# Square roots of the first six norm groups on GpSimd, by a power, in place of a logarithm and an exponential on ScalarE

## The chip, the cores and the metric

The kernel runs on one core of one Trainium2 chip. A core has five engines that work beside each other, each with its own queue of instructions that it takes in order: TensorE (PE: matmuls; its weight loads are listed apart as PEld), VectorE (DVE), ScalarE (ACT), GpSimd (POOL) and SyncE (SP, here only an issuer of DMAs). They wait for each other through semaphores. The metric is the time of one execution on the device in microseconds, lower is better; it is given as the median of three runs.

## The reference

Cosine attention, then a feed-forward layer with an exact GELU. There are 8 batches, 12 heads, 448 positions and a head dimension of 64, all in float32; `tau` is 0.1.

```python
q_n = q / (np.linalg.norm(q, axis=-1, keepdims=True) + 1e-06)
k_n = k / (np.linalg.norm(k, axis=-1, keepdims=True) + 1e-06)
scores = np.matmul(q_n, k_n.transpose(0, 1, 3, 2)) / tau
attn = exp(scores - max) ; attn = attn / (np.sum(attn, axis=-1, keepdims=True) + 1e-09)
x = (attn @ v), heads side by side          # 3584 tokens x 768
out = gelu(x @ w_in) @ w_out                # w_in 768 x 2048, w_out 2048 x 768
```

The change concerns the first two lines: the square root in the norm of each row of q and k.

## The kernel before

**Tiling.** Four heads of one batch make a group `g` of the attention; there are 24, three to a batch. A group's q and k are loaded as one tile `qk` of 128 partitions x (q or k, head pair, 7 chunks, 64). The norms are made in units: unit 0 and unit 1 are the two head pairs of group 0, and unit u above that is group u - 1 (line 116). Units are put together in norm groups n (line 118): norm groups 0 to 4 are units 0 to 4, and norm group 5 is units 5 and 6 together. So a norm group has 14 norms in each partition for n = 0 and 1, 28 for n = 2, 3 and 4, and 56 for n = 5.

**The norm chain.** For each unit: `load_qk` (DMA), `square` (on ACT in the opening, later on POOL), `reduce` (DVE sums 64 squares into `nq`), `logs` and `roots` (ACT: `lq` = Ln(nq + 1e-30), then Exp(0.5 lq) into every second column of a tile `root`, whose other column holds 1e-6), `inverses` (DVE adds the two columns into `se` and takes the reciprocal `rn`), `scale` (POOL multiplies q or k by `rn` into `qkb`, bf16), `transposes` (PE through PSUM for units 0 to 4, and then `copies` by DVE into `qkT`; one DMA from SP's queue for later units). Then `scores` (PE, `st`), `exps` (ACT, `pt`), `sums` and `values` (PE), and `normalise` (DVE) into `x`.

**The rest.** `mm` multiplies `x` by `w_in` into PSUM (`hp`), `gelu` (ACT) writes `g`, and `run` takes the next piece of the product of `g` and `w_out` (`op`), 16 steps over the hidden dimension to an output tile. The weights `wi` and `wo` and the values `v` are loaded by DMAs that POOL issues, so these issues stand in POOL's queue among the multiplications.

**What sets the order.** The function `opening` (line 538) writes out by hand the order of all work of the first three batches: each call in it appends its instructions to the queue of its engine, in this order, and an engine never passes an instruction that waits. For the batches after that, `first` and `attention` do the same by rules; the change does not touch them. [...] Logarithm and exponential share one set (`EXP_SET`) and the GELU has another (`GELU_SET`); `table` puts a table load in ACT's queue. In the opening the logs and roots of norm groups 0 to 4 stand where `EXP_SET` is loaded anyway, and those of norm group 5 stand inside the GELUs of batch 0, between a load of `EXP_SET` and a load of `GELU_SET` (lines 770 to 775).

PE runs a few matmuls that compute nothing (`spin`) in the opening. PSUM tiles of `mm_tile` come from two banks by turns; the transposes of unit 4 and the `hp` tiles 14 and 11 of batch 0 use the same two banks one after the other.

Of the kernel before, what the change touches and what calls it, by code (L numbers as in the profile page):

```python
# [9 lines left out]
F32 = mybir.dt.float32  # L10
BF16 = mybir.dt.bfloat16
AF = mybir.ActivationFunctionType
ALU = mybir.AluOpType
# [3 lines left out]
def kernel(  # L17
# [17 lines left out]
    nc = tc.nc  # L35
    B, H, S, D = q.shape
    C = S // D
# [10 lines left out]
    consts = ctx.enter_context(tc.tile_pool(name="consts", bufs=1))  # L48
# [34 lines left out]
    nc.vector.memset(ones2[64:128, :, 1], 1.0)  # L83
    tiny = consts.tile([128, 1], F32)
    nc.vector.memset(tiny, 1e-30)
    g_first = gp.tile([128, KF, 2 * S], BF16, tag="g", name="g0")
    blank = g_first[:, 0, :S]
    nc.vector.memset(blank, 0.0)

    root2 = [consts.tile([128, 4 * C, 2], F32, name=f"root2_{n}") for n in range(2)]  # L90
# [7 lines left out]
    EXP_SET = "natural_log_exp_and_others"  # L98
    GELU_SET = "gelu_and_others"
# [18 lines left out]
    groups = [[n] for n in range(NQ + 2)] + [[NQ + 2, NQ + 3], [2 * NQ + 1], [2 * NQ + 2]]  # L118
# [3 lines left out]
    shapes = [[len(gr), 2, units[gr[0]][2] - units[gr[0]][1], C] for gr in groups]  # L122
    place = {u: (n, j) for n, gr in enumerate(groups) for j, u in enumerate(gr)}
    qk_t, v_t, sq_t, nq_t, rn_t, qkb_t, qkT_t, pt_t = {}, {}, {}, {}, {}, {}, {}, {}
# [17 lines left out]
    def load_v(n):  # L142
        g, m = v_parts[n]
        t = vp.tile([128, m, 2, C, D], BF16, tag="v", name=f"v{g}")
        for j in range(m):
            v_t[g + j] = t[:, j]
        v_quads(t, g, 0, 1 if g == NQ else m)
        if g == NQ:
            v_rest.append((t, g, 1, m))
# [27 lines left out]
    def reduce(u, part=None):  # L177
        g, s0, s1 = units[u]
        n, j = place[u]
        if n not in nq_t:  # L180
            nq_t[n] = nrm.tile([128, len(groups[n]), 2, s1 - s0, C], F32, tag="nq", name=f"nq{n}")
        for i in range(2) if part is None else (part,):
            nc.vector.tensor_reduce(nq_t[n][:, j, i], sq_t[g, i][:, s0:s1], mybir.AxisListType.X, ALU.add)  # L183

    ln_t, sr_t = {}, {}

    def logs(n):
        nq = nq_t.pop(n)
        ln_t[n] = nrm.tile(list(nq.shape), F32, tag="lq", name=f"lq{n}")
        nc.scalar.activation(ln_t[n], nq, AF.Ln, bias=tiny)  # L190

    def roots(n):
        ln = ln_t.pop(n)
        sr_t[n] = root2[2 if len(groups[n]) == 2 else n % 2][:, :math.prod(shapes[n])]
        nc.scalar.activation(sr_t[n][:, :, 0], ln.rearrange("p j i s c -> p (j i s c)"), AF.Exp, scale=0.5)  # L195
# [10 lines left out]
    def root(n):  # L206
        logs(n)
        roots(n)
        inverses(n)

    def scale(u, parts=None):
        g, s0, s1 = units[u]
        n, j = place[u]
        rn = rn_t[n][:, j]
        if g not in qkb_t:
            qkb_t[g] = qkbp.tile([128, 2, C, 2, D], BF16, tag="qkb", name=f"qkb{g}")
        qkb, t = qkb_t[g], qk_t[g]
        for eng, i in parts or ((nc.gpsimd, 0), (nc.gpsimd, 1)):
            eng.tensor_tensor(  # L219
                qkb[:, i, :, s0:s1].rearrange("p c s d -> p s c d"), t[:, i, s0:s1],  # L220
                rn[:, i].to_broadcast([128, s1 - s0, C, D]), ALU.mult)
# [3 lines left out]
    def transposes(u, i=None):  # L225
        g, s0, s1 = units[u]
        qkb = qkb_t[g]
        if g not in qkT_t:
            qkT_t[g] = qkTp.tile([128, 2, C, 128], BF16, tag="qkT", name=f"qkT{g}")
        if i is None:  # L230
            nc.sync.dma_start_transpose(out=qkT_t[g].rearrange("p i c s -> p (i c) s"),
                                        in_=qkb.rearrange("p i c s d -> p (i c s d)"))
            return
        tp = tp_t[u, i] = mm_tile(f"tp{u}_{i}", (128, C, 128), BF16)
        for c in range(C):
            nc.tensor.transpose(tp[64 * s0:64 * s1, c, :], qkb[:, i, c, s0:s1].rearrange("p s d -> p (s d)"), ident)  # L236

    def copies(u, i):
        g, s0, s1 = units[u]
        rows = slice(64 * s0, 64 * s1)  # L240
        nc.vector.tensor_copy(qkT_t[g][rows, i], tp_t.pop((u, i))[rows])
# [5 lines left out]
    def scores(g, banks, p=None):  # L247
        qkT = qkT_t[g]
        if p is None:
            p = st_turn[0]  # L250
            st_turn[0] ^= 1
        st = pair(p, f"st{g}_{banks[0][1]}")
        for n, (s, c) in enumerate(banks):
            rows = slice(64 * s, 64 * (s + 1))
            for h in range(2):
                cols = slice(64 * h, 64 * (h + 1))
                nc.tensor.matmul(st[cols, n, :S], lhsT=qkT[rows, 1, c, cols], rhs=qkT[rows, 0, :, cols],  # L257
                                 start=True, stop=True, tile_position=(64 * s, 64 * h))
        st_t[g, banks[0]] = st
# [56 lines left out]
    def sums(g, chunks=range(C), p=None):  # L316
        for c in chunks:
            if c == 0:
                bank_t[g, "sm"] = ps_acc.tile([128, 512], F32, tag="sm", name=f"sm{g}") if g < NQ else \
                    pair(p, f"sm{g}")[:, 0]  # L320
            for s in range(2):
                if g < NQ:
                    nc.tensor.matmul(bank_t[g, "sm"][64 * s:64 * (s + 1), :S],  # L323
                                     lhsT=ones2.rearrange("p a h r -> p (a h r)"), rhs=pt_t[g, s, c],
                                     start=(c == 0), stop=(c == C - 1), tile_position=(0, 64 * s))
                    continue

                half = 2
                for i in range(2) if c == half else ((c - (c > half)) % 2,):
                    r = 32 * (2 * s + i)  # L330
                    cols = slice(i * S // 2, (i + 1) * S // 2) if c == half else slice(0, S)
                    nc.tensor.matmul(bank_t[g, "sm"][r:r + 32, cols], lhsT=ones, rhs=pt_t[g, s, c][:, cols],  # L332
                                     start=(c < 2), stop=(c >= C - 2), tile_position=(0, r))

    def values(g, chunks=range(C), p=None):
        for c in chunks:
            if c == 0 and g < NQ and p is None:
                bank_t[g, 0] = ps_acc.tile([128, 512], F32, tag="o", name=f"o{g}_0")
                bank_t[g, 1] = mm_tile(f"o{g}_1")
            elif c == 0:  # L340
                o = pair(p, f"o{g}")
                bank_t[g, 0], bank_t[g, 1] = o[:, 0], o[:, 1]
            for s in range(2):
                for h in range(2):
                    rows, cols = slice(64 * h, 64 * (h + 1)), slice(64 * s, 64 * (s + 1))
                    nc.tensor.matmul(bank_t[g, h][cols, :S], lhsT=v_t[g][rows, s, c, :],  # L346
                                     rhs=pt_t[g, s, c][rows], start=(c == 0), stop=(c == C - 1),
                                     tile_position=(64 * h, 64 * s))
# [113 lines left out]
    def load_wi(i):  # L462
        n = min(i, NQ - 1)
        half = d_ff // 2
        cols = slice(0, d_ff) if n < NQ - 1 else slice((i - n) * half, (i - n + 1) * half)
        for s in range(2):
            nc.gpsimd.dma_start(
                out=wi[64 * s:64 * (s + 1), 2 * n:2 * n + 2, cols],
                in_=moe_w_in[:, cols].rearrange("(n s h d) f -> n s d h f", s=2, h=2, d=D)[n, s])
# [30 lines left out]
    def table(name):  # L500
        nc.scalar.preload_act_table_set(name)
# [5 lines left out]
    def bank(b, m):  # L507
        hps_t[b, m] = mm_tile(f"hp{b}_{m}")[:, :S]
# [11 lines left out]
    def gelu(b, m):  # L520
        sb, hf = divmod(b, 2)
        nc.scalar.activation(g_t[sb][:, m, hf * S:(hf + 1) * S], hps_t.pop((b, m)), AF.Gelu)  # L522
# [15 lines left out]
    def opening():  # L538
# [11 lines left out]
        reduce(0, K)  # L550
        square(1, ((AC, Q),))
        load_v(0)
        logs(0)
        reduce(1, Q)
        roots(0)
        load_wi(0)
        square(1, ((AC, K),))
        inverses(0)
        square(2, ((AC, Q),))
        reduce(1, K)  # L560
        scale(0, ((GP, 1),))
        logs(1)
        reduce(2, Q)
        roots(1)
        scale(0, ((GP, 0),))
        spin(2)
        transposes(0, 1)
# [15 lines left out]
        load_v(1)  # L583
        transposes(1, 1)
        copies(1, 0)
        logs(2)
        scores(0, ((0, 2), (0, 3)))
        roots(2)
        load_wi(1)
        exps(0, ((0, 0), (0, 1)))  # L590
        inverses(2)
# [17 lines left out]
        sums(0, (0,))  # L609
        copies(2, 0)  # L610
        scores(0, ((1, 4), (1, 5)))
        logs(3)
        scores(0, ((0, 6), (1, 6)))
        roots(3)
        transposes(2, 1)
        exps(0, ((1, 4), (1, 5)))
        inverses(3)
# [97 lines left out]
        square(6, ((GP, Q),))  # L715
        reduce(5, Q)
        reduce(4, Q)
        logs(4)
        sums(2, (4,))
        sums(2, (5,))  # L720
        sums(2, (6,))
        roots(4)
        values(2, (5,))
        values(2, (6,))
        banks(0, 2, 0)
# [41 lines left out]
        load_wo(2)  # L767
        gelu(0, 1)
        bank(0, 14)
        table(EXP_SET)  # L770
        reduce(6, K)
        reduce(5, K)
        logs(5)
        roots(5)
        table(GELU_SET)
        gelu(0, 12)
        gelu(0, 10)
        inverses(5)
# [657 lines left out]
```

## Time and profile before

| | us |
|---|---|
| median of 3 runs | 391.75 (391.03 to 391.83) |
| span of the profiled execution | 390.6 |
| PE busy in the span | 382.6 (98%) |
| DVE busy | 273.0 (70%) |
| ACT busy | 269.9 (69%) |
| POOL busy | 248.7 (64%) |

The profile is of one execution; its span runs from its first to its last instruction, and it is the only time that is recorded for that execution. What a run's time holds beyond it is taken as the difference between the median and the span. A line of a timeline gives the start and the duration in us, the engine and the source line, the operation, the tile written and the tiles read, the shape, how many instructions are merged, and in brackets how long the engine had been idle and what ended it.

### The profile page before, as it was taken

The page shows a single profiled execution, that of the slowest core. Times are in us where ns is not written, and L with a number is a line of the kernel's source. Part 1 is how long each engine was busy: PE and PEld are TensorE (multiplying, and loading weights), DVE is VectorE, ACT ScalarE, POOL GpSimd, SP SyncE. Part 2 cuts the span into 40 slices and gives each one's busy share as a digit, 9 for nine tenths or more (in the row PEclk, how much of TensorE's full clock was granted, in tenths as well). Part 3 has the DMA queues.
Part 4 walks back from the last instruction along what each step waited for, and adds up shares of the span by engine and source line. Part 5 has one row for each costly group of instructions (what it writes and reads, how often), then busy time and mean ns, then how long its engine had stood idle before and what let it go on. Part 6 is the DMA issues. An engine that isn't in the chain of part 4 may idle for free.

```text
span 390.6 us, 13166 instructions
## 1 busy us (share of the span) xinstructions
PE 382.6 (98%) x5820; PEld 236.6 (61%) x5820; DVE 273.0 (70%) x509; ACT 269.9 (69%) x391; POOL 248.7 (64%) x161
## 2 busy tenths in 40 slices
PE   7899999999999999999999999999999999999996
PEld 3444568555777656865567556775567555655674
DVE  4878439876778896879696896889685993670032
ACT  5895789857999958996678767997577646504300
POOL 4796950557998399969594794969595770910000
PEclk9999999999999999999999999999999999999999
DMA  8999999926899691889067490876045600130033
GB/s 265 264 262 229 176 191 329 254 56 157 179 203 299 112 217 69 185 158 275 5 172 130 120 243 2 185 131 118 3 91 81 154 9 2 44 82 2 7 79 83
DMA packets 64473, 54.85 MB, mean 140 GB/s; under 512 B 38688, under 2 KB 60320, under 8 KB 64416
## 3 DMA queue, kind: packets, MB, share of 16 engines
q1 hardware_dynamic: 54464, 41.79, 42.0%
q0 software_dynamic: 9568, 11.80, 18.5%
q8 instruction: 45, 0.74, 0.8%
q10 hardware_dynamic: 384, 0.43, 0.4%
q14 instruction: 12, 0.10, 0.1%
HBM read 45.61 MB, written 11.01 MB: 145 GB/s over the span
## 4 chain that ended last, share of the span: by engine, by line
PE 95%; DMA 2%; SPq 1%; ACT 1%; issue 0%; DVE 0%; ACTq 0%
PE hp L493 37%; PE op L427 36%; PE st L257 9%; PE o L346 8%; DMA qk<-in_k_dram 2%; PE op L451 1%; PE sm L323 1%; PE sm L332 1%; PE tp L236 1%; SPq L134 1%; ACT sq L173 0%; ACT pt L267 0%; PE spin L489 0%; DVE last L454 0%; ACT root L195 0%
## 5 line engine op out<-in xcount | busy, mean ns | idle before, releaser
L427 PE MATMUL op<-wo,g 64*64 64x384 bf16 x3456 | 167.1, 323 | 0.2 <-issue 0.2
L267 ACT ACTIVATE pt<-st 128x896 bf16<-128x896 f32 x168 | 147.2, 918 | 19.6 <-PE st L257 17.5
L493 PE MATMUL hp<-x,wi 128*128 128x448 bf16 x768 | 147.0, 353 | 0.0
L427 PEld LDWEIGHTS <-g 64*64 64x64 bf16 x3456 | 106.2, 107 | 40.9 <-issue 4.2
L493 PEld LDWEIGHTS <-wi 128*128 128x128 bf16 x768 | 74.3, 98 | 71.6 <-issue 3.2
L219 POOL TENSOR_TENSOR qkb<-qk,rn 128x896 bf16<-128x896 f32 (+1 forms) x49 | 80.4, 1662 | 46.0 <-DVE rn L203 37.9
L278 POOL TENSOR_TENSOR acc<-acc,pt 128x896 f32<-128x896 f32 x55 | 103.8, 1888 | 4.3
L436 DVE TENSOR_REDUCE ot<-op 128x384 f32<-128x768 f32 x50 | 47.3, 946 | 54.7 <-PE op L427 47.5
L1357 ACT ACTIVATE g<-hp 128x448 bf16<-128x448 f32 x96 | 46.2, 547 | 55.1 <-PE hp L493 55.1
L257 PE MATMUL st<-qkT 64*64 64x448 bf16 x672 | 62.8, 352 | 0.5 <-ACT pt L267 0.5
L183 DVE TENSOR_REDUCE nq<-sq 128x14 f32<-128x896 f32 (+1 forms) x50 | 50.4, 1036 | 13.6 <-ACT sq L173 7.1
L380 DVE TENSOR_TENSOR x<-o,rs 128x448 bf16<-128x448 f32 x48 | 27.6, 611 | 22.9 <-PE o L346 21.9
L175 POOL TENSOR_TENSOR sq<-qk 128x896 f32<-128x896 f32 x16 | 26.6, 1685 | 23.8 <-DMA qk<-in_q_dram 13.3
L346 PE MATMUL o<-pt,v 64*64 64x448 bf16 x672 | 39.5, 349 | 0.0
L290 DVE TENSOR_TENSOR acc<-acc,pt 128x896 f32<-128x896 f32 x30 | 33.0, 1099 | 1.0
L173 ACT ACTIVATE sq<-qk 128x896 f32<-128x896 f32 (+1 forms) x33 | 28.8, 901 | 4.4 <-DMA qk<-in_q_dram 3.2
L257 PEld LDWEIGHTS <-qkT 64*64 64x64 bf16 x672 | 23.1, 106 | 11.7 <-issue 3.7
L375 DVE STREAM_TRANSPOSE rs<-rc 128x448 f32<-128x448 f32 x48 | 28.1, 621 | 0.4
L278 POOL TENSOR_TENSOR acc<-pt 128x896 f32<-128x896 bf16 x11 | 20.7, 1878 | 10.9 <-ACT pt L267 10.9
L346 PEld LDWEIGHTS <-v 64*64 64x64 bf16 x672 | 21.1, 107 | 9.2 <-issue 0.2
L522 ACT ACTIVATE g<-hp 128x448 bf16<-128x448 f32 x32 | 15.4, 547 | 12.8 <-PE hp L493 12.7
L295 DVE TRANSPOSE_TENSOR_REDUCE sa<-acc 128x28 f32<-128x896 f32 x17 | 18.8, 1104 | 0.2
(54 smaller groups left out, 176.0 us busy)
## 6 DMA issues: line engine op xcount, KB each, us to landing
qk<-in_q_dram SPq DMA_DIRECT2D x23, 448.0 KB, 4.9
qk<-in_k_dram SPq DMA_DIRECT2D x23, 448.0 KB, 5.8
out_dram<-ot SPq DMA_DIRECT2D x48, 192.0 KB, 4.0
v<-in_v_dram POOLq DMA_DIRECT2D x6, 672.0 KB, 7.2
wo<-in_moe_w_out_dram POOLq DMA_DIRECT2D x4, 768.0 KB, 10.6
wi<-in_moe_w_in_dram POOLq DMA_DIRECT2D x4, 512.0 KB, 13.8
out_dram<-ot SPq DMA_DIRECT2D x12, 96.0 KB, 2.1
wi<-in_moe_w_in_dram POOLq DMA_DIRECT2D x4, 256.0 KB, 14.1
```

The costliest lines, as they stand in the source:

```text
L173: eng.activation(sq, t, AF.Square)
L183: nc.vector.tensor_reduce(nq_t[n][:, j, i], sq_t[g, i][:, s0:s1], mybir.AxisListType.X, ALU.add)
L219: eng.tensor_tensor(qkb[:, i, :, s0:s1].rearrange("p c s d -> p s c d"), t[:, i, s0:s1], rn[:, i].to_broadcast([128, s1 - s0, C, D]), ALU. ...
L257: nc.tensor.matmul(st[cols, n, :S], lhsT=qkT[rows, 1, c, cols], rhs=qkT[rows, 0, :, cols], start=True, stop=True, tile_position=(64 * s, 6 ...
L267: nc.scalar.activation(pt, st[:, :, :S], AF.Exp, scale=inv_tau)
L278: nc.gpsimd.tensor_tensor(acc_t[g], all_t[g][:, 0] if c == 1 else acc_t[g], all_t[g][:, c], ALU.add)
L290: nc.vector.tensor_tensor(acc_t[g], acc_t[g], all_t[g][:, c], ALU.add)
L346: nc.tensor.matmul(bank_t[g, h][cols, :S], lhsT=v_t[g][rows, s, c, :], rhs=pt_t[g, s, c][rows], start=(c == 0), stop=(c == C - 1), tile_po ...
L427: nc.tensor.matmul(ps[cols, r, :NH], lhsT=g_t[sb][rows, kf, t * 128 + 64 * c:t * 128 + 64 * (c + 1)], rhs=wo[rows, kf, ni * NH:(ni + 1) * NH],
L436: nc.vector.tensor_reduce(part, ps[:, :, :NH].rearrange("p r d -> p d r"), mybir.AxisListType.X, ALU.add)
L493: nc.tensor.matmul(t, lhsT=wi[:, kd, m * 128:(m + 1) * 128], rhs=x_t[b][:, kd, :], start=(kd == 0), stop=(kd == KD - 1))
L1357: nc.scalar.activation(g_t[sb][:, m, hf * S:(hf + 1) * S], hps.pop(m), AF.Gelu)
```

## The change

The norm groups 0 to 5 get their roots by a new function `powers`, which is one POOL instruction: `nq` raised to the power of a constant tile `halves` that holds 0.5, written to the same column of the same `root` tile. The calls of `logs` and `roots` for these groups go, and with those of norm group 5 the two table loads around them. `powers(n)` stands where `roots(n)` stood. Norm groups 6 and later keep the logarithm and the exponential.

```diff
+    halves = consts.tile([128, 8 * C], F32)
+    nc.vector.memset(halves, 0.5)
...
+    def powers(n):
+        nq = nq_t.pop(n)
+        m = math.prod(shapes[n])
+        sr_t[n] = root2[2 if len(groups[n]) == 2 else n % 2][:, :m]
+        nc.gpsimd.tensor_tensor(sr_t[n][:, :, 0], nq.rearrange("p j i s c -> p (j i s c)"), halves[:, :m], ALU.pow)
...
         load_v(0)
-        logs(0)
         reduce(1, Q)
-        roots(0)
+        powers(0)
         load_wi(0)
...
         scale(0, ((GP, 1),))
-        logs(1)
         reduce(2, Q)
-        roots(1)
+        powers(1)
         scale(0, ((GP, 0),))
...
-        logs(2)
         scores(0, ((0, 2), (0, 3)))
-        roots(2)
+        powers(2)
         load_wi(1)
...
-        logs(3)
         scores(0, ((0, 6), (1, 6)))
-        roots(3)
+        powers(3)
...
-        logs(4)
         sums(2, (4,))
         sums(2, (5,))
         sums(2, (6,))
-        roots(4)
+        powers(4)
...
         bank(0, 14)
-        table(EXP_SET)
         reduce(6, K)
         reduce(5, K)
-        logs(5)
-        roots(5)
-        table(GELU_SET)
+        powers(5)
```

POOL's queue in the opening, from the first load of `v` to the scales of unit 3 (group 2), before the change; `rn` with another number is that of another norm group:

```order
L155 DMA v_180<-in_v_dram 128x2x448
L467 DMA wi<-in_moe_w_in_dram 64x2x2048 x2
L219 TENSOR_TENSOR qkb_197<-qk_133,rn_192 128x7x64 x2
L219 TENSOR_TENSOR qkb_197<-qk_133,rn_221 128x7x64 x2
L155 DMA v_260<-in_v_dram 128x4x448
L467 DMA wi<-in_moe_w_in_dram 64x2x2048 x2
L219 TENSOR_TENSOR qkb_297<-qk_139,rn_285 128x2x7x64 x2
L219 TENSOR_TENSOR qkb_364<-qk_142,rn_360 128x2x7x64
```

The same place with the change (the new lines of code move the line numbers by 2 to 8):

```order
L157 DMA v_182<-in_v_dram 128x2x448
L198 TENSOR_TENSOR root_0_127<-nq_178,halves 128x14
L475 DMA wi<-in_moe_w_in_dram 64x2x2048 x2
L227 TENSOR_TENSOR qkb_197<-qk_135,rn_192 128x7x64
L198 TENSOR_TENSOR root_1_128<-nq_184,halves 128x14
L227 TENSOR_TENSOR qkb_197<-qk_135,rn_192 128x7x64
L227 TENSOR_TENSOR qkb_197<-qk_135,rn_219 128x7x64 x2
L157 DMA v_258<-in_v_dram 128x4x448
L198 TENSOR_TENSOR root_0_127<-nq_199,halves 128x28
L475 DMA wi<-in_moe_w_in_dram 64x2x2048 x2
L227 TENSOR_TENSOR qkb_293<-qk_141,rn_281 128x2x7x64 x2
L198 TENSOR_TENSOR root_1_128<-nq_295,halves 128x28
```

Four powers have come into the queue: one ahead of the first `wi` issues, one between the two halves of the first scale, one ahead of the second `wi` issues, and one behind the scales that the third made possible.

POOL's queue further on, at batch 0's `hp` matmuls, before the change: two loads of `wo` in a row, between the scales of unit 4 and those of units 6 and 5.

```order
L175 TENSOR_TENSOR sq_0_631<-qk_319 128x896
L175 TENSOR_TENSOR sq_1_691<-qk_319 128x896
L219 TENSOR_TENSOR qkb_726<-qk_168,rn_697 128x2x7x64 x2
L473 DMA wo<-in_moe_w_out_dram 128x4x768 x2
L219 TENSOR_TENSOR qkb_815<-qk_319,rn_786 128x2x7x64
```

With the change:

```order
L177 TENSOR_TENSOR sq_0_625<-qk_315 128x896
L198 TENSOR_TENSOR root_0_127<-nq_567,halves 128x28
L177 TENSOR_TENSOR sq_1_683<-qk_315 128x896
L227 TENSOR_TENSOR qkb_718<-qk_170,rn_689 128x2x7x64 x2
L481 DMA wo<-in_moe_w_out_dram 128x4x768
L198 TENSOR_TENSOR root_0_129<-nq_627,halves 128x56
L481 DMA wo<-in_moe_w_out_dram 128x4x768
L227 TENSOR_TENSOR qkb_803<-qk_315,rn_774 128x2x7x64
```

The power of norm group 4 stands between the squares of unit 6, and that of norm group 5 between the two loads of `wo`. DVE's and PE's queues keep their order; on ACT twelve activations and two table loads are gone.

## The prediction

> **What bounds the kernel now.** I read the page first, then the busy time by stages, then each engine's timeline of the opening. The page says that TensorE (PE) is almost never idle.
>
> ```profile
> span 390.6 us, 13166 instructions
> PE 382.6 (98%) x5820; PEld 236.6 (61%) x5820; DVE 273.0 (70%) x509; ACT 269.9 (69%) x391; POOL 248.7 (64%) x161
> ```
>
> A share over the whole span hides where the idle lies, so the same by stages (start:end, length, then busy us and count of each engine, granted clock, DMA share, GB/s):
>
> ```profile
> 0.00:15.00 15.00, 10.84 (x64) 5.08 (x66) 8.41 (x27) 9.23 (x17) 8.72 (x18) 1.00 0.92 269
> 15.00:33.30 18.30, 18.29 (x235) 8.36 (x235) 14.80 (x25) 17.09 (x22) 17.07 (x14) 1.00 1.09 256
> 33.30:52.00 18.70, 18.70 (x116) 9.93 (x116) 8.64 (x16) 12.01 (x22) 15.54 (x11) 1.00 1.09 194
> 52.00:380.00 328.00, 327.81 (x5337) 208.32 (x5340) 238.89 (x440) 231.55 (x332) 207.36 (x119) 1.00 0.56 127
> ```
>
> PE loses 4.2 us in the first 15 us and 0.2 us in the next 365. Two things follow. After 15 us nothing that ScalarE (ACT) is relieved of can shorten the kernel unless PE's own queue gets going earlier; and a delay that reaches PE early is not made up later, since there is no idle time to eat it. From 15 to 33 us ACT is nearly as full as PE. Its timeline (start, duration, instruction, idle before):
>
> ```profile
> 13.52 0.30 ACT L190 ACTIVATE lq<-nq,tiny 128x28 f32<-128x28 f32 x1
> 13.85 0.23 ACT L195 ACTIVATE root<-lq 128x28 f32<-128x28 f32 x1
> 13.99 4.13 ACT L267 ACTIVATE pt<-st 128x896 bf16<-128x896 f32 x5
> 17.97 0.35 ACT L190 ACTIVATE lq<-nq,tiny 128x28 f32<-128x28 f32 x1
> 18.35 0.23 ACT L195 ACTIVATE root<-lq 128x28 f32<-128x28 f32 x1
> 18.48 1.71 ACT L267 ACTIVATE pt<-st 128x896 bf16<-128x896 f32 x2
> 20.35 12.07 ACT L267 ACTIVATE pt<-st 128x896 bf16<-128x896 f32 x14 [0.16 <-PE st L257]
> ```
>
> The fourteen exponentials of attention groups 1 and 2 run from 20.35 to 32.42 without a gap, so when the first of them starts decides when PE comes to the dense `hp` matmuls at 33.3 us. The two log and root pairs ahead of them cost ACT 13.99 - 13.52 = 0.47 and 18.48 - 17.97 = 0.51 us (each from the log's start to the next exponential's). Now GpSimd (POOL) in the same stretch:
>
> ```profile
> 5.77 0.89 POOL L155 DMA_DIRECT2D v<-in_v_dram  x1
> 6.65 1.22 POOL L467 DMA_DIRECT2D wi<-in_moe_w_in_dram  x2
> 7.86 1.86 POOL L219 TENSOR_TENSOR qkb<-qk,rn 128x448 bf16<-128x448 f32 x2
> 10.86 1.83 POOL L219 TENSOR_TENSOR qkb<-qk,rn 128x448 bf16<-128x448 f32 x2 [1.15 <-DVE rn L203]
> 12.64 0.83 POOL L155 DMA_DIRECT2D v<-in_v_dram  x1
> 13.46 1.20 POOL L467 DMA_DIRECT2D wi<-in_moe_w_in_dram  x2
> 14.84 3.33 POOL L219 TENSOR_TENSOR qkb<-qk,rn 128x896 bf16<-128x896 f32 x2 [0.19 <-DVE rn L203]
> 19.39 1.69 POOL L219 TENSOR_TENSOR qkb<-qk,rn 128x896 bf16<-128x896 f32 x1 [1.21 <-PE tp L236]
> ```
>
> POOL is the engine that makes the scaled q and k, which PE must transpose, and it is nearly full: from 10.86 to 18.17 it pauses for 0.19 us. The change puts the roots into this queue, in order, where ACT had run them beside it.
>
> **What one power costs.** No row shows a power on any engine. The nearest rows are POOL's own multiplications in two sizes (count, busy us, mean ns of one):
>
> ```profile
> L219 POOL TENSOR_TENSOR qkb<-qk,rn 128x896 bf16<-128x896 f32 x45 | 76.7, 1726 | 44.9 <-DVE rn L203 36.8 <-ACT pt L267 6.5 <-PE tp L236 1.2
> ...
> L219 POOL TENSOR_TENSOR qkb<-qk,rn 128x448 bf16<-128x448 f32 x4 | 3.7, 951 | 1.1 <-DVE rn L203 1.1
> ```
>
> Their difference gives (1726 - 951) / 448 = 1.73 ns an element, and 951 - 775 = 0.18 us fixed. Call the power's time a for 14 elements, b for 28, c for 56. The lower bound is a power at the price of one multiplication: a 0.20, b 0.23, c 0.28. Upwards I count steps: a power is a logarithm, a product and an exponential, each a chain of multiplications and additions, with range handling. As an estimate I take 30 such steps at 1.73 ns, 52 ns an element: a = 0.18 + 0.73 = 0.91, b = 1.64, c = 3.09. My upper bound is 70 steps, 121 ns: a 1.87, b 3.57, c 6.96. The count of steps is a choice; the multiplication's own price is the cheap end, and I leave it because a power can't be one multiplication.
>
> [...]
>
> **The sum, step by step.** Norm groups 0 and 1 (14 elements each). On POOL the first power stands behind the v load and before the two wi issues, so `scale(0)` of k starts at 7.86 + a; the second power stands between the two halves of `scale(0)`. Both halves and both powers end at 9.72 + 2a. `scale(1)` then had 1.15 us to wait for its reciprocal, and this pause takes in 2a up to 1.15. What is left is d = max(0, 2a - 1.15) = 0.67 us. On VectorE (DVE) `inverses(1)` waits for the second power, with the copies of attention group 0's transposes queued behind it; this ends before the pause does.
>
> Norm groups 2 and 3 (28 each). From the end of `scale(1)` POOL has: v issue to 13.46 + d, the power b, wi issues 1.20, `scale(2)` 3.33, the power b again. Sum: 13.46 + 1.20 + 3.33 = 17.99, plus d + 2b. Before, ACT ended this last root at 18.35 + 0.23 = 18.58. So the root of norm group 3 comes d + 2b - 0.59 = 0.67 + 3.28 - 0.59 = 3.36 us later. The 0.59 is what POOL loses in waits today. Who waits for that root:
>
> ```profile
> 18.61 0.21 DVE L201 TENSOR_REDUCE se<-root 128x28 f32<-128x56 f32 x1 [0.34 <-ACT root L195]
> 18.93 0.33 DVE L203 RECIPROCAL rn<-se 128x28 f32<-128x28 f32 x1
> 19.17 0.60 DVE L241 COPY qkT<-tp 128x896 bf16<-128x896 bf16 x1
> ```
>
> ```profile
> 19.91 0.71 PE L257 MATMUL st<-qkT 64*64 64x448 bf16 x8
> ```
>
> DVE works in order: `inverses(3)` holds the copy of attention group 1's second transpose, and the copy's end at 19.77 releases that group's first scores at 19.91, which release the run of fourteen exponentials. There is no slack in this chain, so all 3.36 us pass to ACT at 20.35 and to PE at 33.3. What ACT saves, 0.47 + 0.51 us, only lets attention group 0's exponentials end sooner; then ACT waits. `inverses(2)` likewise holds a copy for attention group 0's later scores, but by b + d, less than what follows.
>
> Norm group 4 (28). Its power stands between two squares, ahead of a pause for data:
>
> ```profile
> 34.25 1.68 POOL L175 TENSOR_TENSOR sq<-qk 128x896 f32<-128x896 f32 x1 [0.97 <-DVE rc L371]
> 38.00 1.68 POOL L175 TENSOR_TENSOR sq<-qk 128x896 f32<-128x896 f32 x1 [2.08 <-DMA qk<-in_k_dram]
> ```
>
> The pause takes in 2.07 us, more than b: nothing, and POOL even comes b - 2.07 = -0.43 us back against PE's shift. If b exceeded it, POOL would be that much later still.
>
> Norm group 5 (56 elements) and the two table loads. The power stands between the two issues of the last wo loads.
>
> ```profile
> 42.92 1.56 POOL L473 DMA_DIRECT2D wo<-in_moe_w_out_dram  x2
> ```
>
> ```profile
> 43.43 0.27 DVE L201 TENSOR_REDUCE se<-root 128x56 f32<-128x112 f32 x1 [1.64 <-ACT root L195]
> 43.74 0.50 DVE L203 RECIPROCAL rn<-se 128x56 f32<-128x56 f32 x1
> 47.13 1.15 DVE L241 COPY qkT<-tp 128x896 bf16<-128x896 bf16 x2 [2.89 <-PE tp L236]
> ```
>
> ```profile
> 47.32 4.70 PE L493 MATMUL hp<-x,wi 128*128 128x448 bf16 x24
> ...
> 54.31 1.47 PE L427 MATMUL op<-wo,g 64*64 64x384 bf16 x32
> ...
> 61.59 0.57 PE L257 MATMUL st<-qkT 64*64 64x448 bf16 x8
> ```
>
> The reciprocal of norm group 5 would end at about 43.70 + c + 0.84 = 47.63, and behind it on DVE stand the copies that free the banks of the seventh `hp` matmul, at 47.32 + 6 x 0.19 = 48.46; one copy takes 0.58, so it must start by 47.88. With POOL's -0.43 the slack is about 0.7 us: hidden, but just; beyond it each us of c costs one. Two more covers lie here:
>
> ```profile
> DMA to landing us min/median/max: 7.3/8.8/10.3
> ```
>
> ```profile
> 51.91 5.06 SPq L231 DMA_TRANSPOSE qkT<-qkb  x2
> ```
>
> ```profile
> qkT<-qkb SPq DMA_TRANSPOSE x2, 5.9
> ```
>
> The first row is for the two wo loads: issued at 42.92 and 43.70, they land at 50.2 and 54.0, 3.8 apart, so the second queues behind the first and a later issue mostly costs nothing; it is used at 54.31. The DMA transposes on SP's queue, behind the scales that wait for this reciprocal, land 5.9 after 51.91, at 57.8, and are used at 61.59: 3.8 us of cover against c - 0.43 + 0.1 = 2.8.
>
> ```profile
> L501 ACT ACT_TABLE_LOAD x9 | 11.5, 1283 | 1.3 <-PEq L1417 1.2
> ```
>
> Two table loads go, 2 x 1.28 us of ACT, in a stage where PE is busy 18.70 of 18.70 us: worth nothing. `halves` is one more DVE memset before PE's filler matmuls: nothing.
>
> Total: 390.6 + 3.4 = 394.0 us of span. The median of 391.75 lies 1.15 above the span, so the time is 395.1 us.
>
> **The rivals.** A difference below 0.2%, 0.78 us, cannot be told from none here.
> - *The power is nearly a multiplication.* With up to 10 steps (18 ns; b 0.68, a 0.43, d 0) the sum is at most 0.78, at the lower bound 0.46 - 0.59 = -0.13: 391.6 to 392.5 us. For it: the one price on POOL that the trace has. Against it: a power has more to do. Chance 0.21, and not slower.
> - *ACT's relief decides.* If ACT's 0.98 us reached PE, 390.8 us. It would need norm group 3's root by 17.6, when POOL is still in `scale(2)`, and PE would meet the wo load, which lands 0.3 us before its use. 0.04.
> - *The first power loads code.* It would add to a of norm group 0, one for one as d is open. The nearest loading row is the table load's 1.28: 396.4 us. Against it: POOL's first two multiplications take 1.86, the next two 1.83. [...] 0.08.
> - *The power is far dearer.* At 121 ns d is 2.59, the chain gives 2.59 + 7.14 - 0.59 = 9.1, and the copies behind norm group 5's reciprocal come late too, by 6.96 + 0.84 + 1.50 - 4.18 = 5.1 us: 391.75 + 14.2 = 406 us. At 260 ns (a 3.82, b 7.46, c 14.74) the same terms give about 429. Beyond 121 ns: 0.12.
>
> **How the numbers follow.** My forecast, 18 to 121 ns, has 0.55 and is slower: 392.5 to 406 us, likeliest 395.1. Slower is 0.55 + 0.08 + 0.12 = 0.75, within 0.2% 0.21, faster 0.04. The range runs from the multiplication's price to 70 steps, 391.5 to 406, and leaves out some 0.15.
>
> **What would show it.** The powers appear as POOL rows of 14, 28 and 56 elements, whose differences give the price of an element. If I am right, `se` of norm group 3 waits for POOL, the first score of attention group 1 moves from 19.91 to about 23.3, ACT waits before the run of fourteen, and PE's time after 33.3 us is unchanged in length. I am wrong if the powers are below 0.7 us at 28 elements, if the stage from 33.3 to 52 lengthens at c near 3, or if PE's scores come later and the end does not.

## The result: 418.5 us, 7% slower

The changed kernel takes 418.54 us (median of 4 runs, 417.72 to 420.49) against 391.6 us of the kernel before beside it: a ratio of 1.069, 95% interval 1.066 to 1.072. The prediction had 395.1 and a range up to 406. The direction and the places were right; the sizes were not, and one cost, TensorE's clock, was not in the sum. The ratios, here and below, leave out executions that were slower at a lower clock, which is why a few of the ranges below reach far up.

### The profile after

The page of the changed kernel: span, then busy time, share and count of each engine.

```profile
span 417.0 us, 13162 instructions
PE 394.7 (95%) x5820; PEld 240.4 (58%) x5820; DVE 273.2 (66%) x510; ACT 265.6 (64%) x377; POOL 277.4 (67%) x167
```

PE has the same 5820 matmuls as before, but is busy for 12.1 us more: matmuls that do the same work take longer somewhere. POOL has 28.7 us more, ACT 4.3 less. By stages (start:end, length, busy us and count of each engine, granted clock, DMA share, GB/s); the stages end where the run of 70 `hp` matmuls starts and where the first `op` starts, which was at 33.29 and 51.95 before:

```profile
0.00:48.29 48.29, 38.30 (x296) 16.31 (x297) 23.24 (x52) 26.39 (x31) 41.01 (x36) 0.75 0.81 195
48.29:76.61 28.32, 21.21 (x112) 10.54 (x108) 8.60 (x16) 7.73 (x16) 28.01 (x13) 0.88 0.70 118
76.61:417.00 340.39, 335.21 (x5417) 213.57 (x5416) 241.40 (x444) 231.44 (x331) 208.34 (x120) 1.00 0.53 124
```

The same stages before:

```profile
0.00:33.29 33.29, 29.12 (x297) 13.43 (x297) 23.20 (x51) 26.32 (x38) 25.79 (x31) 1.00 1.01 262
33.29:51.95 18.66, 18.66 (x112) 9.89 (x108) 8.65 (x16) 11.96 (x22) 15.54 (x11) 1.00 1.09 195
51.95:390.60 338.65, 334.82 (x5417) 213.31 (x5416) 241.15 (x444) 231.60 (x332) 207.36 (x119) 1.00 0.55 126
```

The opening is 48.29 - 33.29 = 15.0 us longer, the stage behind it 28.32 - 18.66 = 9.7, the rest 340.39 - 338.65 = 1.7; together the 26.4 us by which the span grew. What is new stands in the eighth column: PE's granted clock, 1.00 in every stage before, is 0.75 and 0.88 here.

The powers by size, from the groups of the changed kernel (count, busy us, mean ns of one, idle before):

```profile
L198 POOL TENSOR_TENSOR root<-nq,halves 128x28 f32<-128x28 f32 x3 | 14.5, 4821 | 0.2 <-DVE nq L185 0.2
L198 POOL TENSOR_TENSOR root<-nq,halves 128x56 f32<-128x56 f32 x1 | 9.3, 9322 | 0.0
L198 POOL TENSOR_TENSOR root<-nq,halves 128x14 f32<-128x14 f32 x2 | 5.2, 2623 | 0.0
```

An element costs (4821 - 2623) / 14 = 157 ns and (9322 - 4821) / 28 = 161 ns. So a, b and c of the prediction are 2.62, 4.82 and 9.32 us, where it took 0.91, 1.64 and 3.09. They lie in POOL's queue where the prediction put them; POOL's timeline (start, duration, instruction):

```profile
6.33 2.63 POOL L198 TENSOR_TENSOR root<-nq,halves 128x14 f32<-128x14 f32 x1
...
11.05 2.61 POOL L198 TENSOR_TENSOR root<-nq,halves 128x14 f32<-128x14 f32 x1
...
26.68 4.83 POOL L198 TENSOR_TENSOR root<-nq,halves 128x28 f32<-128x28 f32 x1
...
60.04 9.32 POOL L198 TENSOR_TENSOR root<-nq,halves 128x56 f32<-128x56 f32 x1
```

The first power takes 2.63 us and the second 2.61: nothing is paid for the first use. The root of norm group 3 ends at 26.68 + 4.83 = 31.51, against 18.58 before. DVE's timeline shows who stands behind it, and behind that of norm group 5:

```profile
31.54 0.21 DVE L209 TENSOR_REDUCE se<-root 128x28 f32<-128x56 f32 x1 [4.17 <-POOL root L198]
31.79 0.33 DVE L211 RECIPROCAL rn<-se 128x28 f32<-128x28 f32 x1
32.03 0.56 DVE L249 COPY qkT<-tp 128x896 bf16<-128x896 bf16 x1
...
69.39 0.27 DVE L209 TENSOR_REDUCE se<-root 128x56 f32<-128x112 f32 x1 [11.35 <-POOL root L198]
69.70 0.50 DVE L211 RECIPROCAL rn<-se 128x56 f32<-128x56 f32 x1
70.12 1.08 DVE L249 COPY qkT<-tp 128x896 bf16<-128x896 bf16 x2
```

PE's timeline then shows what these copies release, and the waits that PE did not have before:

```profile
11.16 0.58 PE L244 MATMUL tp<-ident,qkb 128*64 128x128 bf16 x7 [2.00 <-POOL qkb L227]
...
14.62 0.95 PE L244 MATMUL tp<-ident,qkb 128*64 128x128 bf16 x7 [2.59 <-POOL qkb L227]
...
32.65 0.96 PE L265 MATMUL st<-qkT 64*64 64x448 bf16 x8 [1.67 <-DVE qkT L249]
...
48.29 13.42 PE L501 MATMUL hp<-x,wi 128*128 128x448 bf16 x70
62.33 1.30 PE L501 MATMUL hp<-x,wi 128*128 128x448 bf16 x6
70.73 5.96 PE L501 MATMUL hp<-x,wi 128*128 128x448 bf16 x18 [7.11 <-DVE qkT L249]
76.61 2.14 PE L435 MATMUL op<-wo,g 64*64 64x384 bf16 x48
```

The chain is the one of the prediction: root, `se`, reciprocal, copy, scores of attention group 1 at 32.65 (19.91 before). The scores come 12.7 us later, `hp` 15.0. Within the stage behind it stands one stall of 7.11 us, at the bank that the copies behind norm group 5's reciprocal free. And something is slow that waits for nothing: the 7 transposes at 11.16 take 0.58 us, the 7 at 14.62 take 0.95; the last 18 `hp` take 5.96 us where 24 took 4.70. The changed kernel in five short stretches (columns as above: PE's busy time behind the length, the granted clock third from the end):

```profile
14.00:15.00 1.00, 0.38 (x4) 0.38 (x5) 0.63 (x2) 0.00 (x0) 1.00 (x2) 0.58 1.04 212
15.00:38.00 23.00, 19.66 (x128) 7.95 (x130) 9.81 (x17) 9.53 (x11) 21.92 (x15) 0.50 0.87 189
38.00:39.00 1.00, 1.00 (x20) 0.34 (x12) 0.23 (x1) 0.76 (x2) 0.99 (x2) 0.97 1.07 184
...
68.00:69.00 1.00, 0.00 (x0) 0.00 (x0) 0.00 (x0) 0.00 (x0) 1.00 (x1) 0.89 0.00 0
69.00:75.00 6.00, 4.27 (x12) 1.72 (x12) 1.77 (x4) 1.42 (x3) 5.71 (x6) 0.50 0.72 114
```

The clock falls in the second of the two waits of 2.00 and 2.59 us, between 14 and 15 us, and PE runs at half of it up to 38 us. It falls again within the stall of 7.11 us, between 68 and 69, and PE works at half clock for some 5 us behind the stall.

### The profile page after: what moved, and what is told of

Its sections match the earlier page's. It is cut to its first block, busy times and chain, and to the rows that moved or that the text cites. A ratio compares the mean times of both kernels' runs of the same rounds, so it can differ in the third digit from the quotient of the medians.

```text
span 417.0 us, 13162 instructions
## 1 busy us (share of the span) xinstructions
PE 394.7 (95%) x5820; PEld 240.4 (58%) x5820; DVE 273.2 (66%) x510; ACT 265.6 (64%) x377; POOL 277.4 (67%) x167
## 3 DMA queue, kind: packets, MB, share of 16 engines
q1 hardware_dynamic: 54464, 41.79, 38.2%
## 4 chain that ended last, share of the span: by engine, by line
PE 84%; POOL 10%; issue 2%; DVE 2%; DMA 1%; SPq 0%; POOLq 0%
PE op L435 34%; PE hp L501 32%; PE st L265 8%; PE o L354 7%; POOL root L198 6%; POOL qkb L227 2%; PE op L459 1%; DMA qk<-in_k_dram 1%; PE sm L340 1%; POOL sq L177 1%; PE sm L331 1%; POOL wo L481 1%; PE tp L244 1%; POOL wi L475 1%; DVE nq L185 0%
## 5 line engine op out<-in xcount | busy, mean ns | idle before, releaser
L501 PE MATMUL hp<-x,wi 128*128 128x448 bf16 x768 | 149.6, 356 | 7.1 <-DVE qkT L249 7.1
L265 PE MATMUL st<-qkT 64*64 64x448 bf16 x672 | 66.9, 366 | 3.3 <-DVE qkT L249 3.3
L354 PE MATMUL o<-pt,v 64*64 64x448 bf16 x672 | 40.9, 357 | 0.0
L175 ACT ACTIVATE sq<-qk 128x896 f32<-128x896 f32 (+1 forms) x33 | 28.7, 901 | 3.9 <-DMA qk<-in_q_dram 2.3
L198 POOL TENSOR_TENSOR root<-nq,halves 128x28 f32<-128x28 f32 (+2 forms) x6 | 29.0, 4839 | 0.3 <-DVE nq L185 0.2
L354 PEld LDWEIGHTS <-v 64*64 64x64 bf16 x672 | 22.2, 109 | 9.7 <-issue 1.2
```

The source lines that it names most:

```text
L198: nc.gpsimd.tensor_tensor(sr_t[n][:, :, 0], nq.rearrange("p j i s c -> p (j i s c)"), halves[:, :m], ALU.pow)
L501: nc.tensor.matmul(t, lhsT=wi[:, kd, m * 128:(m + 1) * 128], rhs=x_t[b][:, kd, :], start=(kd == 0), stop=(kd == KD - 1))
```

## The experiments

The theory after the result has two parts. *Price*: the power costs 157 to 161 ns an element on POOL, and the prediction's own formulas with this price give most of the loss. *Clock*: the new waits let PE's granted clock fall to 0.50, and that costs time beyond the waits. Rivals: the *place* (a foreign instruction in POOL's queue and the roots' new engine cost time whatever the price), the *chain* alone (half clock beside waits costs nothing), and, for norm group 5, that undoing the one stall gives its time back.

| kernel | us, median (range) | before there | ratio, 95% interval | 70 `hp` start at | stall before the last `hp` |
|---|---|---|---|---|---|
| after_again, the change | 418.84 (417.87 to 419.46) | 391.75 | 1.071, 1.068 to 1.074 | 48.35 | 7.10 |
| e1_mult | 392.53 (391.82 to 398.0) | 392.45 | 1.002, 0.999 to 1.004 | 32.59 | none |
| e2_only5 | 397.99 (396.64 to 402.48) | 392.45 | 1.018, 1.011 to 1.026 | 32.03 | 4.28 |
| e3_not5 | 408.87 (408.41 to 409.55) | 392.45 | 1.044, 1.042 to 1.047 | 47.73 | none |
| e4_spins | 417.87 (416.49 to 418.72) | 392.45 | 1.067, 1.063 to 1.070 | 46.34 | 7.55 |
| e4b_spins | 416.03 (415.1 to 416.7) | 391.75 | 1.063, 1.060 to 1.066 | 46.13 | 7.55 |
| e5_cover5 | 420.64 (419.21 to 421.42) | 391.75 | 1.075, 1.071 to 1.079 | 48.99 | none |
| e7_only01 | 402.51 (401.67 to 403.57) | 391.75 | 1.029, 1.026 to 1.032 | 43.59 | none |
| e9_01fill | 396.36 (396.15 to 399.06) | 391.55 | 1.014, 1.010 to 1.018 | 37.16 | none |
| e10_only23 | 402.53 (401.12 to 403.44) | 391.55 | 1.028, 1.025 to 1.031 | 42.79 | none |
| e6_only4 | 393.22 (391.55 to 398.73) | 391.55 | 1.0045, 1.001 to 1.008 | 32.29 | none |

The kernels ran in three groups, each on one chip beside the kernel before, and are read against the median of before of their own group.

> The changed kernel once more, beside the next three on the same chip: 418.5 us by every theory. GpSimd's powers again 2.6, 4.8 and 9.3 us, TensorE's granted clock 0.50 from about 14.5 to 38 us and again for some 6 us near 70.

The change run again, unedited, gives 418.84 us: its loss, the stall and the late `hp` are those of the first profile. So is the half clock, but for one stretch: from about 31.4 to 34.8 us it is back at 1.00 here (0.84 from 30 to 35 us; 8 `st` take 0.57 us at 33.13, and 0.96 at 32.65 in the first profile).

### The price without the place, e1_mult

```diff
-        nc.gpsimd.tensor_tensor(sr_t[n][:, :, 0], ..., halves[:, :m], ALU.pow)
+        nc.gpsimd.tensor_tensor(sr_t[n][:, :, 0], ..., halves[:, :m], ALU.mult)
```

> The six powers are multiplications by 0.5 at the same places of GpSimd's queue (the roots then hold half the sum of squares: the square root is left out). Theory 'price': what costs is the time of each power, 2.62, 4.83 and 9.32 us at 14, 28 and 56 elements. With 0.20, 0.23 and 0.28 us by the multiplication's rows the prediction's own sum gives -0.13 us: 391.5 us, same as before, no wait of TensorE over 1 us after 15 us, granted clock 1.00 throughout. Rival 'place': the cost comes from standing in GpSimd's queue and from the new waits on it, whatever the instruction computes: then over 395 us.

No change: 1.002, interval 0.999 to 1.004. The group of 28 elements, and PE's timeline in this kernel:

```profile
L198 POOL TENSOR_TENSOR root<-nq,halves 128x28 f32<-128x28 f32 x3 | 0.7, 244 | 0.0
```

```profile
32.59 13.41 PE L501 MATMUL hp<-x,wi 128*128 128x448 bf16 x70
...
55.32 1.49 PE L435 MATMUL op<-wo,g 64*64 64x384 bf16 x32 [1.54 <-DMA wo<-in_moe_w_out_dram]
```

A multiplication of 28 elements at the same place takes 0.244 us where the power takes 4.82, twenty times as much, and with it the kernel takes its old time. The place is cleared; the whole loss is the power's price and what follows from it. The second row looks like the prediction's rival on ACT's relief: `hp` comes 0.7 us earlier, and PE then meets the load of wo and waits 1.54 us. But this profile is of an execution of 396.12 us, and in e2_only5 and e6_only4, where ACT keeps the logs and roots of norm groups 0 to 3, `hp` comes earlier still (32.03 and 32.29). ACT's `square` waits 3.2 us for loads of q in the first 90 us of the profile before, and 1.8 in e6_only4. So the 33.29 of before is one execution's value, and a difference of 1 us in it needs no edit to explain it.

### Norm group 5 alone and all but it, e2_only5 and e3_not5

```diff
 e2_only5: powers(5) stays, for the others
-        powers(0) ... powers(4)
+        logs(0), roots(0) ... logs(4), roots(4), where before.py had them
 e3_not5: powers(0) to powers(4) stay
-        powers(5)
+        table(EXP_SET); logs(5); roots(5); table(GELU_SET), where before.py had them
```

> Only norm group 5 keeps the power; groups 0 to 4 are back on ScalarE. Theory 'price': the copies behind this norm group's reciprocal start at 43.70 + 9.32 + 0.84 = 53.9 in place of 47.9 at the latest, so TensorE stands still for 6.0 us before the seventh hp matmul; if the stand halves its clock for some 3 to 5 us, 2 us more: 397.5 to 400 us. The rest of the program unchanged in length. Rival 'all from the opening': the 28-element powers start everything and this one only inherits it: under 394 us.

> Norm groups 0 to 4 keep the power; group 5 is back on ScalarE with its two table loads. Theory 'price': the opening is as late as with the change (hp matmuls at 48.3 in place of 33.3, 15.0 us), and the 9.7 us that the stage of batch 0's hp matmuls lost are back: about 408.5 us. Rival 'one cause': if the stand in the later stage comes from the late opening, it stays, and the time is over 415 us.

Both times came out by the price theory, 397.99 and 408.87 us. PE's timeline of the first and of the second:

```profile
46.06 1.30 PE L501 MATMUL hp<-x,wi 128*128 128x448 bf16 x6
51.64 4.86 PE L501 MATMUL hp<-x,wi 128*128 128x448 bf16 x18 [4.28 <-DVE qkT L249]
```

```profile
47.73 13.42 PE L501 MATMUL hp<-x,wi 128*128 128x448 bf16 x70
61.77 4.70 PE L501 MATMUL hp<-x,wi 128*128 128x448 bf16 x24
```

With the power of norm group 5 alone the opening keeps its time and the stall at the seventh `hp` of the run of 24 is there; without it the stall is gone, the 24 take their 4.70 us again, and the opening is as late as with the whole change. The stall belongs to norm group 5, the 14 to 15 us of the opening to norm groups 0 to 4. In the first kernel the stall is 4.28 us, and not the 6.0 expected: POOL starts the power at 40.92, 8.89 us behind the start of the 70 `hp`, where the expectation had 43.70 - 33.29 = 10.41, because POOL's waits ahead of two squares are shorter in this execution (1.46 us in all against 0.97 and 2.08 before). The 18 `hp` behind it take 4.86 us instead of 18/24 x 4.70 = 3.53; 4.28 + 1.33 = 5.6 us is the loss of 5.5 us.

### Keeping the clock, e4_spins and e4b_spins

Filler matmuls of PE (`spin`) at the places where the changed kernel's PE waits, 38 in e4_spins and 62 in e4b_spins; they write a bank that nobody reads.

```diff
-        spin(20)
+        spin(29)
...
         inverses(1)
-        spin(1)
+        spin(13)
         transposes(0, 0)
...
-        spin(1)
+        spin(9)      # 24 in e4b_spins
         scores(0, ((1, 0), (1, 1)))
...
         sums(0, (4,))
+        spin(9)      # 18 in e4b_spins
         scores(1, ((0, 0), (1, 0)))
```

> All six powers stay; 37 more filler matmuls stand where TensorE waits in the opening (9 before the first transposes, 12 before the second, 8 and 8 before the two scores that wait for copies). They compute nothing that is used. Theory 'clock': 2.3 us of the opening's 15.0 are TensorE at a granted clock of 0.50 from 14.5 to 38 us, because it idled; with the fillers the clock stays near 1.00 there and the hp matmuls start near 46 us: 416 to 416.5 us. Rival 'chain alone': the waits for the powers set every start, the clock costs nothing: 418.5 us or more.

> All six powers, and 62 more filler matmuls where TensorE waits in the opening, so that it has work until each wait ends (9, 12, 23 and 17). Theory 'clock': the granted clock stays at 1.00 to the hp matmuls, which start at 46.0 us in place of 48.3 while the powers end when they did; the end comes about 2 us earlier than in the changed kernel of the same chip. Rival 'chain alone': the hp matmuls still start at 48.3 us and the time is the changed kernel's.

The first try kept the clock at 1.00 only up to about 25 us (0.99 from 20 to 25, 0.50 from 25 to 30), behind a wait of 2.93 us that was left and ended at 23.63; its 417.87 us lies between the two expectations. The second holds it to the `hp`; its stages and its PE timeline:

```profile
0.00:30.00 30.00, 25.65 (x163) 12.13 (x164) 11.54 (x31) 13.26 (x16) 25.24 (x23) 1.00 0.97 251
30.00:46.00 16.00, 14.73 (x197) 6.80 (x195) 11.58 (x20) 12.65 (x15) 15.14 (x13) 1.00 0.55 115
```

```profile
46.13 13.41 PE L501 MATMUL hp<-x,wi 128*128 128x448 bf16 x70
...
69.02 5.71 PE L501 MATMUL hp<-x,wi 128*128 128x448 bf16 x18 [7.55 <-DVE qkT L249]
```

`hp` starts 48.35 - 46.13 = 2.2 us earlier than in the change run beside it (after_again), and the kernel takes 2.8 us less (416.03 against 418.84). More matmuls make it faster: the half clock does cost in the opening. It costs little there because most of the 23 us stand beside longer waits for the powers. POOL moves with PE, but not as far: its power of norm group 5 starts at 58.32 instead of 60.09, 1.77 us earlier, as its wait of 1.13 us for DVE's `nq` is gone. So the stall grows by 0.45 us.

### One cover mended, e5_cover5

The copies that free the banks go ahead of norm group 5's reciprocal on DVE, and the last load of wo ahead of its power on POOL.

```diff
+        copies(4, 1)
+        copies(4, 0)
+        load_wo(3)
         powers(5)
...
-        load_wo(3)
...
-        copies(4, 1)
...
-        copies(4, 0)
```

> All six powers; the copies of unit 4's transposes go ahead of norm group 5's reciprocal on VectorE, and both last wo loads ahead of its power on GpSimd. Theory 'covers in a row': the 7.1 us before the seventh hp matmul go, but the power still ends at 70 us, so the scales of units 5 and 6 and the DMA transpose behind them land near 84 us, and the first scores of attention group 3's successor, wanted at 61.6 + 15.0 = 76.6, wait some 7.5 us there: 416 to 418 us. Rival 'the copies alone': with the copies free that stage is whole again: 409 us.

The stall is gone, and the kernel is no faster: 420.64 us against 418.84, and above the 416 to 418 expected. PE's timeline shows what took its place:

```profile
79.92 1.07 PE L435 MATMUL op<-wo,g 64*64 64x384 bf16 x12 [2.37 <-DVE ot L442]
87.63 0.96 PE L265 MATMUL st<-qkT 64*64 64x448 bf16 x8 [6.64 <-DMA qkT<-qkb]
```

Behind the same power stand the scales and, behind these, the DMA transposes of the next scores. The prediction had counted this cover (3.8 us) as the one after the copies. With c at 9.32 us both are used up, and mending the first shows the second. Beside it the clock is 0.50 again between 80 and 90 us, and PE waits 2.37 us for `ot`, which was not foreseen; how the 1.8 us on top divide between these is not settled.

### Norm groups 0 and 1 alone, e7_only01 and e9_01fill

```diff
 e7_only01: powers(0) and powers(1) stay
-        powers(2) ... powers(5)
+        logs(2), roots(2) ... logs(5), roots(5), with the table loads, where before.py had them
 e9_01fill: e7_only01 and
-        spin(20)
+        spin(29)
...
-        spin(1)
+        spin(13)
         transposes(0, 0)
```

> Only norm groups 0 and 1 keep the power (2.62 us each). Theory 'price': GpSimd comes to scale(1) by 2 x 2.62 - 1.15 = 4.1 us late; scale(2) still has a pause of 0.19 and 0.37 us of slack before its transposes, so group 1's first scores come 3.4 to 3.7 us late, and TensorE's half clock after the wait adds 1 to 2 us: 395 to 397.5 us. Rival 'only norm groups 2 and 3 matter', since the reciprocal of norm group 1 is not waited for on the path: under 393.5 us.

> Powers for norm groups 0 and 1 alone, the other four roots on ScalarE, and 21 fillers of TensorE more: nine ahead of the opening's first weights and twelve ahead of the first transposes, where TensorE waited 2.0 and 2.6 us before its granted clock fell to 0.50. Clock theory (without the fillers this kernel lost 10.3 us up to the first hp product, of which GpSimd's delay is 3.2 to 4 and the rest the half clock): with the clock kept at 1.00 the first hp product starts near 37 and the time is 395 to 396.5 us. Rival, the chain: the 10.3 us come from GpSimd's later scale alone, the fillers only fill, and the time stays at 402 to 403 us.

The first was a miss: 402.51 us, 5 us above the 395 to 397.5 expected. POOL was only as late as expected (`scale(2)` starts at 19.04 instead of 14.84, 4.2 us later), but `hp` came 43.59 - 33.29 = 10.3 us later. The stretch from 15 to 25 us of e7_only01, and then of e9_01fill:

```profile
15.00:25.00 10.00, 9.94 (x52) 4.09 (x53) 5.49 (x9) 4.63 (x7) 7.06 (x7) 0.50 1.09 243
```

```profile
15.00:25.00 10.00, 9.65 (x90) 4.37 (x91) 7.12 (x12) 7.48 (x13) 8.82 (x9) 1.00 1.10 246
```

PE is busy 9.94 of 10 us in the first and gets through 52 matmuls at a clock of 0.50; in the second it is busy 9.65 and gets through 90. ACT shows how this reaches the end; its timeline in the first and in the second kernel:

```profile
18.33 0.92 ACT L275 ACTIVATE pt<-st 128x896 bf16<-128x896 f32 x1
20.09 0.92 ACT L275 ACTIVATE pt<-st 128x896 bf16<-128x896 f32 x1 [0.85 <-PE st L265]
21.84 0.92 ACT L275 ACTIVATE pt<-st 128x896 bf16<-128x896 f32 x1 [0.82 <-PE st L265]
```

```profile
17.79 4.13 ACT L275 ACTIVATE pt<-st 128x896 bf16<-128x896 f32 x5
...
22.35 13.94 ACT L275 ACTIVATE pt<-st 128x896 bf16<-128x896 f32 x16
```

With the fillers five exponentials run without a gap in 4.13 us; without them they stand 1.75 us apart and wait for PE's scores. `hp` starts at 37.16 instead of 43.59, and the kernel takes 396.36 us. That is the clock theory's 395 to 396.5, and outside the chain's 402 to 403. The half clock is worth 6.4 us here, more than the 3.87 us of delay that called it up (37.16 - 33.29; the prediction's formula for d gives 2 x 2.62 - 1.15 = 4.09; against the 32.29 of e6_only4 the delay is 4.87).

### Norm groups 2 and 3 alone, norm group 4 alone: e10_only23 and e6_only4

```diff
 e10_only23: powers(2) and powers(3) stay; e6_only4: powers(4) stays
-        the other powers
+        the logs, roots and table loads of before.py in their place
```

> Powers for norm groups 2 and 3 alone. Price theory: they stand one behind the other on GpSimd, nothing is late ahead of them, so root 3 comes 2 x 4.83 - 0.59 = 9.1 us later, the first hp product too, and the time is 400 to 402 us if TensorE's clock stays, with up to 2 us on top if TensorE waits long enough there for its clock to be halved. Rival, the fixed part: most of the 12.9 us that root 3 lost in the full change came from norm groups 0 and 1 ahead of it and from the clock, and this kernel loses 5 us or less: 397 us or under.

> Power for norm group 4 alone. Covers theory: its 4.83 us go into the 2.07 us pause of GpSimd that follows and into the covers behind it that norm group 5's power used up in the full change, so the time is 391.5 to 392.7 us, no change. Rival, no cover: every power on GpSimd is paid for in full beyond the pause, 4.83 - 2.07 = 2.8 us, and the time is 394.3 to 395 us.

e10_only23 takes 402.53 us. POOL's timeline, then PE's:

```profile
21.99 4.83 POOL L198 TENSOR_TENSOR root<-nq,halves 128x28 f32<-128x28 f32 x1
```

```profile
18.81 0.96 PE L265 MATMUL st<-qkT 64*64 64x448 bf16 x4 [4.21 <-DVE qkT L249]
...
27.96 0.96 PE L265 MATMUL st<-qkT 64*64 64x448 bf16 x8 [1.68 <-DVE qkT L249]
```

The root of norm group 3 ends at 26.82, 8.2 us later than before, where the price theory had 9.1; the scores of attention group 1 come 27.96 - 19.91 = 8.1 later, and `hp` 42.79 - 33.29 = 9.5. Behind the wait of 4.21 us the clock is at half here too (0.81 from 15 to 20 us, 0.50 from 20 to 30), which goes with the 1.4 us between the two. The rival's 5 us or less is out.

e6_only4 does not decide. POOL's timeline and PE's:

```profile
33.92 4.85 POOL L198 TENSOR_TENSOR root<-nq,halves 128x28 f32<-128x28 f32 x1
```

```profile
32.29 13.41 PE L501 MATMUL hp<-x,wi 128*128 128x448 bf16 x70
46.32 4.70 PE L501 MATMUL hp<-x,wi 128*128 128x448 bf16 x24
```

In the profiled execution (391.7 us) 4.85 us of power make no stall: the 24 `hp` take 4.70. (PE waits 0.85 us for wo behind them, having come 1.0 us earlier than in the profile before.) But the median lies between the two theories, and the interval of the ratio, 0.1 to 0.8%, is 0.5 to 3.0 us. That the covers take in this power is what the trace shows; that it is entirely free is not shown.

## Why the prediction was wrong

**The step that failed is the price of the power.** "As an estimate I take 30 such steps at 1.73 ns, 52 ns an element … My upper bound is 70 steps, 121 ns." It measured 157 to 161 ns, or some 92 such steps. All three terms a, b and c were too small by a factor of three, and with the upper bound the top of the range. The rival "the power is far dearer" (0.12) is what happened. That a power is made of such steps was the author's assumption: no run shows them, only the time of the whole in three sizes.

**The formulas held in the opening, and roughly behind it.** With the measured prices: d = 4.09; the root of norm group 3 later by 4.09 + 2 x 4.83 - 0.59 = 13.16 us (measured 31.51 - 18.58 = 12.93); the copies behind norm group 5's reciprocal late by 9.32 + 0.84 + (4.83 - 2.07) - 4.18 = 8.74 (the stall measured 7.11). Together 391.75 + 21.9 = 413.65 us, so with the right price the prediction would still have been 4.9 us low.

**A term was missing: PE's clock.** The prediction reckoned a wait of PE as its length. Two waits of 2.0 and 2.6 us with little work between them, and one of 7.1, were followed by matmuls at half the clock. In the opening this cost 48.29 - 33.29 - 12.74 = 2.26 us beyond the later scores, and e4b_spins took 2.2 of them back. Behind the stall the 18 `hp` took 5.96 instead of 18/24 x 4.70 = 3.53, 2.4 us; that was not tried by itself. Set against 13.16 + 8.74 = 21.9, the 26.4 us measured are: scores 12.74, half clock 2.26, stall 7.11, half clock behind it and rest 2.55, behind the first `op` 1.74. The stall is shorter than 8.74 for two reasons. POOL's other pause before, the 0.97 us ahead of the square at 34.25 in the prediction's own lines, is gone as well, which leaves 7.77; e4b_spins, with the clock at 1.00, has 7.55. The rest is PE's, which the half clock brings to the stall later.

**The 1.74 us behind the first `op` stay open.** The change run again has 416.1 - 76.72 = 339.4 us there, 0.7 above before, and e4b_spins 413.3 - 74.65 = 338.65, the same as before. It is not a steady effect. Some of it stands between 91 and 100 us, where groups of four `st` matmuls take up to 0.53 us in both profiles of the changed kernel and 0.36 to 0.39 in e4b_spins, at a granted clock of 1.00 in all three; no run explains it.

**Point by point.**
- "There is no slack in this chain": right. Scores come 12.74 us later for a root 12.93 later (8.1 for 8.2 in e10_only23).
- Norm group 4's power costs nothing as long as the 2.07 us pause takes it in, and POOL is later by the excess: in direction right, with e6_only4 inconclusive on the rest.
- Norm group 5 "hidden, but just; beyond it each us of c costs one": the cover is there, and c went far beyond it (e2_only5, e3_not5), but the bound is not a fixed 3.3 us: e2_only5 paid 4.28 of its 9.35 us, so 5.1 were covered. The cover of the DMA transposes behind it was also used up (e5_cover5).
- "PE's time after 33.3 us is unchanged in length": wrong, and through c alone: without norm group 5's power the stage has its 18.7 us (e3_not5). The forecast stood on c near 3; the far dearer rival had the stage lengthen, and it did.
- The rivals: the price of a multiplication would have given no change (e1_mult shows it); ACT's relief is worth nothing that can be measured (e1_mult has it, without the price, and takes its old time); the first power is no dearer than the second (2.63 against 2.61 us).
- Parts do not add up as medians: e7_only01 and e10_only23 each cost 10.8 to 11.0 us, while all of norm groups 0 to 4 cost 16.4 (e3_not5), because the half clock that e7_only01 pays for lies beside the longer waits for the powers when norm groups 2 and 3 are there too.

## What to carry to other kernels

An operation that no row of the trace shows has no price until it is measured; a function such as a power is not bounded by counting steps, and one small kernel with two sizes of it settles more than all working behind it. Find out first from which price on the covers are used up (here 2.07 us of pause for norm group 4, and 47.88 - 43.70 - 0.84 = 3.3 us for norm group 5, though e2_only5 had 5.1: a cover read from one execution can be off by what its loads were late), and say how likely the price lies beyond that. Where a change lets TensorE wait between short bursts (here 2.00 and 2.59 us with 0.9 us of matmuls between), look at the granted clock of the stretch behind (here 0.50), and not at the wait alone: filler matmuls that only keep it busy gave 6 us back in one kernel and 2.8 in another.

## What the runs showed of the hardware

- A power on GpSimd takes 2.62, 4.82 and 9.32 us for 128x14, 128x28 and 128x56 fp32 elements; a multiplication of the same tiles takes 0.226, 0.244 and 0.314 us. ScalarE's logarithm and exponential together held ACT for 0.47 to 0.51 us for 128x28.
- The granted clock of TensorE fell to 0.50 between 14 and 15 us, in the second of two waits of 2.00 and 2.59 us with 0.9 us of matmuls between, and stayed there from 15 to 38 us, 19.66 of which PE was busy; in e7_only01 it stayed at 0.50 though PE was busy for 9.94 of 10 us. In the changed kernel it fell again 5.2 us into the stall of 7.11 us and was back at 1.00 4.9 us after work began again at 70.73; the fall in the opening came without one wait that long. What brought it back at 38 us is not settled: in e9_01fill and e4b_spins, where the waits are filled, it stays at 1.00 up to `hp`, and more they do not show.
- Worked out from the granted clock of rows of half a microsecond (0.67 from 14.0 us, 0.94 from 38.0, 0.78 from 68.5, 0.89 from 75.5), it changes at 14.17, 38.06, 68.78 and 75.61 us in the changed kernel: 23.89 us at 0.50, 30.72 at 1.00 and 6.83 at 0.50, which stand as 7 to 9 to 2; what sets these lengths is not shown. From rows of 5 us the changes come out at about 14.3, 38.2, 68.9 and 75.8 in after_again (beside its stretch at 1.00 from 31.4 to 34.8), and at 24.9, 31.8, 65.9 and 72.7 in e4_spins: the moments differ from execution to execution. PE was busy for 0.88 of the 5.01 us from the start of the first of the two waits, at 9.16, to the fall at 14.17, and for 0.01 of the 5.16 us from the start of the stall to the fall at 68.78. So PE need not be wholly idle for the clock to fall; how little work is enough is not shown.
